# Decay attention and a hard-swish MoE layer: the masked scores stay in PSUM through the exponential, the half precision copy and the low pass

## The chip, the cores and the metric

One core of a Trainium2 chip. The kernel is one launch; its time is the device time of an execution in microseconds (us). A run is compared by the median of several executions. The engines are TensorE (PE; its weight loads are PEld), VectorE (DVE), ScalarE (ACT), GpSimd (POOL), and SyncE (SP), which issues the transfers.

## What is computed

The reference, cut to what matters (batch 8, 8 heads, 576 positions, head size 64; 4608 tokens of width 512, hidden width 2048):

```python
scores = scale * (q @ k.T)                         # scale = 1/8
cum = cumsum(log(clip(f, 1e-4, 1)))
scores = where(causal, -1e9, scores + cum[:, None] - cum[None, :])
attn = exp(scores - max(scores));  attn /= sum(attn) + 1e-9
x = (attn @ v)                                     # heads side by side: 4608 x 512
h = x @ w_in;  g = h * clip(h + 3, 0, 6) / 6
out = g @ w_out
```

## The kernel before

All 64 heads of attention and the whole MoE layer run on one core, one woven into the other. Numbers that need more than half precision are held as a pair of fp16 values, a high part and a low part (value minus high part), and multiplied as high by high, high by low and low by high.

**The visits.** A loop runs over 68 visits: four of kind A, eight of kind B (both for batch 0 only, in another form that the change leaves alone) and 56 of kind F, one for each head of batches 1 to 7. Visit 12 is the first of kind F. Each visit builds the scores of its head in `rows`, in two halves. Half 0 holds the row chunks 1, 4 and 0 (192, 576 and 64 keys wide), half 1 the chunks 2 and 3 (320 and 448 keys). For one half:

1. PE writes the scores of its chunks into the PSUM tile `pn`, 128x1024 fp32, two banks, from a pool of two such tiles (`ps_s`), by the matmuls on L632 and L635. Each visit so uses both tiles once.
2. DVE makes the **product** of each chunk (L643): it scales, adds the causal mask `W` and keeps the row's minimum in `MF`. Before the change the result goes to the SBUF tile `pp`, and `pn` is free when the last chunk has been read. An instruction that reads out the accumulator follows each product.
3. ACT takes the **exponential** of each chunk in place (L652), with the row's `MF` as bias, and then makes the half precision **copy** of it in the SBUF tile `ring` (L669).
4. DVE makes the **low pass** (`low`, L615): value times 16 minus the fp16 copy, written as fp16 to `ring`. It is seven instructions a head: half 0 has 128x128, 128x512, a pair of 64 columns for two chunks, and 64x64; half 1 has 128x256, 128x384 and the pair.
5. SP transposes `ring` into `pT` (L690), from which PE later makes `pav` = attention times values (L715 to L720, function `av`); DVE divides by the row sums (L748 to L750), and a last transpose puts the head into `xT`.

**The MoE layer.** `h_unit` makes 12 matmuls (L804 to L806) into `ph`, ACT applies the Relu to `r` (L812), DVE multiplies (L815, which reads `r` from SBUF and `ph` from PSUM), ACT makes the high part of `gT` (L816) and DVE the low part (L817, both inputs in SBUF). `out_unit` makes 48 matmuls into `po` (L859 to L861), ACT evicts them (L869). The MoE tile of a batch can start when all eight heads of the batch are in `xT`. The weights' own low parts are made on DVE in the first 160 us (L309). POOL prepares the next head's operands by six instructions a visit (L461 to L474), of which two read two SBUF tensors (L471, L474).

**The order.** The generator code interleaves visits and MoE steps; a list scheduler then fixes the order of each engine's instructions when the program is built. Each engine works through its own list strictly in order and waits on semaphores. The dependences are taken from tiles: two instructions on different engines, or two that follow each other on one engine, wait for each other where they touch the same PSUM tile.

## Time and profile before

| | |
|---|---|
| median of 3 runs | 1063.88 us (1058.98 to 1065.66) |
| the profiled execution | 1065.9 us, span in the profile 1064.1 us |
| PE busy | 1025.8 us, 96% |
| DVE busy | 773.5 us, 73% |
| ACT busy | 600.6 us, 56% |
| POOL busy | 423.2 us, 40% |

The span has four parts. From 0 to 143 us the weights and inputs are loaded and the visits of kind A and B run. From 143 to 282 us the first visits of kind F run, beside the MoE tile of batch 0. From 282 to 915 us the other visits run beside the MoE tiles of the batches before them. From 915 us on only MoE work of the last batch is left. A busy time is a union: an instruction that begins before the one ahead of it has ended does not count twice.

### The profile page before, as it was taken

What the parts mean: (1) busy time and instruction counts of PE and PEld (TensorE: products, weight loads), DVE (VectorE), ACT (ScalarE), POOL (GpSimd) and SP (SyncE); (2) the same over time, 40 slices, a digit from 0 to 9 for tenths busy, and PEclk for the clock granted to TensorE, in tenths of its full rate; (3) what the DMA queues carried; (4) which work ended last, traced back from release to release, by engine and by line L of the source; (5) the groups of instructions that cost most, each with busy time, mean ns of one, the idle gap of its engine ahead of it and who ended that gap; (6) DMA issues with size and microseconds to landing.
All of it is one profiled execution on the core that took longest, in us unless ns stands there. A gap on an engine that the chain in (4) does not pass through costs nothing.

```text
span 1064.1 us, 20761 instructions
## 1 busy us (share of the span) xinstructions
PE 1025.8 (96%) x7833; PEld 617.0 (58%) x7833; DVE 773.5 (73%) x1927; ACT 600.6 (56%) x1190; POOL 423.2 (40%) x436
## 2 busy tenths in 40 slices
PE   7799989889999999999999999999999999999998
PEld 5557856755455755555555755555555755545545
DVE  7977898999986679876986689876976788505500
ACT  4786765766664557655654556655743577405500
POOL 8654583665452444443343244444434442000000
PEclk8869999999999999999999999999999999999999
DMA  7765324778455554366444474456444534400000
GB/s 229 256 220 139 101 68 104 162 148 153 118 106 100 117 135 104 78 129 144 90 86 99 101 156 98 96 125 143 86 91 83 103 80 80 82 28 11 1 20 31
DMA packets 248416, 114.35 MB, mean 107 GB/s; under 512 B 224788, under 2 KB 226124, under 8 KB 248316
## 3 DMA queue, kind: packets, MB, share of 16 engines
q1 hardware_dynamic: 248316, 113.03, 46.9%
q8 instruction: 61, 1.00, 0.4%
q14 instruction: 39, 0.32, 0.1%
HBM read 47.93 MB, written 9.73 MB: 54 GB/s over the span
## 4 chain that ended last, share of the span: by engine, by line
PE 69%; DVE 16%; DMA 7%; ACT 4%; issue 3%; SPq 1%; DVEq 0%; ACTq 0%
PE po L859 11%; PE po L861 11%; PE po L860 11%; PE ph L804 7%; PE ph L806 6%; PE ph L805 6%; DVE ring L615 5%; PE pn L635 3%; PE pn L632 3%; DMA vst<-in_vS_dram 2%; DMA ring<-in_w_out_dram 2%; DVE r L815 2%; DVE pp L643 2%; DVE gT L817 2%; DVE w L309 1%
## 5 line engine op out<-in xcount | busy, mean ns | idle before, releaser
L615 DVE SCALAR_TENSOR_TENSOR ring<-pp,ring 128x128 f16<-128x128 f32 x392 | 235.2, 639 | 52.4 <-ACT ring L669 50.4
L461 POOL TENSOR_SCALAR TK<-ST 64x576 fp32r<-64x576 f32 (+1 forms) x68 | 54.3, 799 | 431.0 <-PE pn L632 394.0
L859 PE MATMUL po<-w,gT 128*128 128x512 f16 x560 | 209.6, 382 | 0.0
L804 PE MATMUL ph<-xT,w 128*128 128x512 f16 (+1 forms) x576 | 201.8, 358 | 7.7 <-DVE r L815 7.7
L861 PE MATMUL po<-w,gT 128*128 128x512 f16 x560 | 208.7, 381 | 0.3 <-DVE gT L817 0.3
L860 PE MATMUL po<-w,gT 128*128 128x512 f16 x560 | 208.6, 381 | 0.2 <-DVE w L309 0.2
L806 PE MATMUL ph<-xT,w 128*128 128x512 f16 (+1 forms) x576 | 201.2, 357 | 0.0
L805 PE MATMUL ph<-xT,w 128*128 128x512 f16 (+1 forms) x576 | 201.1, 357 | 0.0
L652 ACT ACTIVATE pp<-pp,MF 128x192 f32<-128x192 f32 x280 | 147.9, 554 | 87.3 <-DVE MF L643 86.1
L643 DVE CUSTOM_DVE_ANT_0 pp<-pn,W 128x192 f32<-128x192 f32 x280 | 123.3, 480 | 20.2 <-PE pn L635 19.9
L632 PE MATMUL pn<-TK,TQ 68*128 68x192 f32 x336 | 125.1, 385 | 5.3 <-DVE MF L643 3.0
L816 ACT CAST gT<-r 128x512 f16<-128x512 f32 (+1 forms) x144 | 81.6, 567 | 79.8 <-DVE r L815 79.1
L669 ACT ACTIVATE ring<-pp 128x192 f16<-128x192 f32 x280 | 119.8, 458 | 1.6
L812 ACT ACTIVATE r<-ph,bias_r,SC 128x512 f32<-128x512 f32 (+1 forms) x144 | 103.4, 720 | 29.2 <-PE ph L806 17.6
L817 DVE TENSOR_TENSOR gT<-r,gT 128x512 f16<-128x512 f32 (+1 forms) x144 | 100.8, 701 | 24.7 <-ACT gT L816 23.2
L815 DVE SCALAR_TENSOR_TENSOR r<-r,ph 128x512 f32<-128x512 f32 (+1 forms) x144 | 88.9, 618 | 40.6 <-ACT r L812 40.6
L635 PE MATMUL pn<-T,T 128*128 128x192 f32 x336 | 115.2, 370 | 0.0
L474 POOL TENSOR_TENSOR T<-ST,T 64x576 fp32r<-64x576 f32 (+1 forms) x68 | 107.3, 1577 | 5.1
L471 POOL TENSOR_TENSOR T<-ST,TQ 64x576 fp32r<-64x576 f32 (+2 forms) x68 | 98.6, 1451 | 5.4
L869 ACT ACTIVATE o<-po,SC 128x512 f32<-128x512 f32 (+1 forms) x37 | 24.7, 669 | 125.1 <-PE po L861 123.7
L861 PEld LDWEIGHTS <-gT 128*128 128x128 f16 x560 | 54.6, 98 | 67.5 <-issue 7.2
L860 PEld LDWEIGHTS <-gT 128*128 128x128 f16 x560 | 54.6, 98 | 59.8 <-issue 5.0
(152 smaller groups left out, 2016.1 us busy)
## 6 DMA issues: line engine op xcount, KB each, us to landing
ST<-in_qk_dram SPq DMA_DIRECT2D x64, 288.0 KB
out_dram<-o SPq DMA_DIRECT2D x33, 256.0 KB
ring<-in_w_out_dram SPq DMA_DIRECT2D x16, 512.0 KB
vst<-in_vS_dram SPq DMA_DIRECT2D x7, 1040.0 KB
ring<-in_w_in_dram SPq DMA_DIRECT2D x9, 512.0 KB
w<-in_w_in_dram SPq DMA_DIRECT2D x7, 512.0 KB
vst<-in_vS_dram SPq DMA_DIRECT2D x14, 130.0 KB
pT<-ring SPq DMA_TRANSPOSE x112
```

The costliest lines, as they stand in the source:

```text
L615: nc.vector.scalar_tensor_tensor(out_, x, PSC, hi, op0=ALU.mult, op1=ALU.subtract)
L632: nc.tensor.matmul(dst, TQ[i][0:D + 4, qs], TK[i][0:D + 4, a:e], start=True, stop=False)
L635: nc.tensor.matmul(dst, T7[j][:, qs], T1[j][:, a:e], start=False, stop=True)
L643: nc.vector.tensor_tensor_reduce(pp[:r, w:w + kw], pn[:r, o:o + kw], W[:r, 4 * P + r - kw:4 * P + r], -0.125, 3.0e38, ALU.add, ALU.min, ac ...
L652: nc.scalar.activation(x_, x_, AF.Exp, bias=mc[:r, e0 + x:e0 + x + 1], scale=-1.0)
L804: nc.tensor.matmul(ph, w1[0][:, cc, fs_], xh, start=(cc == 0), stop=False)
L805: nc.tensor.matmul(ph, w1[0][:, cc, fs_], xl, start=False, stop=False)
L806: d = nc.tensor.matmul(ph, w1[1][:, cc, fs_], xh, start=False, stop=(cc == NCC - 1))
L817: nc.vector.tensor_tensor(gT[:, 1, fc, c0:c1], r, gT[:, 0, fc, c0:c1], op=ALU.subtract)
L859: nc.tensor.matmul(po, g[:, 0, fc, ts_], w2[:, fc, 0, c], start=(fc == 0), stop=False)
L860: nc.tensor.matmul(po, g[:, 0, fc, ts_], w2[:, fc, 1, c], start=False, stop=False)
L861: d = nc.tensor.matmul(po, g[:, 1, fc, ts_], w2[:, fc, 0, c], start=False, stop=(fc == NFC - 1))
```

## The change

The product of each chunk is written back into `pn`, to where the scores stood. The exponential then runs in place in PSUM, and the copy and the low pass read from `pn`; `pp` is gone. In half 1 chunk 2 now lies in the first bank and chunk 3 in the second. Two small tiles that used the buffers of `pp` at the start (`fs`, `lf`) now lie in `xT`.

```diff
@@ decay()
-        fs = p2.tile([NHEAD, S], F32, tag="Pp", name="fs")
+        fs = xT[0].bitcast(F32).rearrange("p a c l t -> p (a c l t)")[0:NHEAD, 0:S]
...
-        lf = p2.tile([NHEAD, S], F32, tag="Pp", name="lf")
+        lf = xT[0].bitcast(F32).rearrange("p a c l t -> p (a c l t)")[0:NHEAD, S:2 * S]
@@
-    PLACE = {1: 0, 4: 192, 0: 768, 3: 0, 2: 512}
+    PLACE = {1: 0, 4: 192, 0: 768, 2: 0, 3: 512}
@@ rows()
-            pp = p2.tile([P, 832], F32, tag="Pp", name=f"pp_{v}_{half}")
-            at, w = {}, 0
+            pp, at = pn, PLACE
             for x, c in enumerate(NAT[half]):
                 o, r, kw = PLACE[c], RR[c], RB[c] + RR[c]
-                at[c] = w
                 nc.vector.tensor_tensor_reduce(
-                    pp[:r, w:w + kw], pn[:r, o:o + kw], W[:r, 4 * P + r - kw:4 * P + r],
+                    pn[:r, o:o + kw], pn[:r, o:o + kw], W[:r, 4 * P + r - kw:4 * P + r],
                     -0.125, 3.0e38, ALU.add, ALU.min, accum_out=mc[:r, e0 + x:e0 + x + 1],
                 )
-                w += kw
```

Three lines fewer: L643, L652, L669 and L690 become L641, L649, L666 and L687, and what stands behind them moves up by three (L804 to L801, L815 to L812, L859 to L856). L632, L635 and L615 stay.

The number of instructions of each kind is the same. Their order is not, and the waits are not. Two places of visit 50, in the steady part of the program, show how. The names in brackets are the semaphores that an instruction waits for: `Activation` is ACT's, `DVE` is DVE's, `DMAHW` a transfer's.

On ACT before, half 0 of visit 50, from the first exponential to the last copy (`ring1` is the half precision tile of this half):

```order
L652 ACTIVATE pp_50_0_8261<-pp_50_0_8261,MF0_169 128x192 [waits DVE_49]
L669 ACTIVATE ring1_186<-pp_50_0_8261 128x192 [waits DMAHW0_49,Activation_49]
L652 ACTIVATE pp_50_0_8261<-pp_50_0_8261,MF0_169 128x576 [waits DVE_49]
L652 ACTIVATE pp_50_0_8261<-pp_50_0_8261,MF0_169 64x64 [waits DVE_49]
L669 ACTIVATE ring1_186<-pp_50_0_8261 128x576 [waits Activation_49]
L812 ACTIVATE r_4_11_0_8280<-ph_4_11_0_8238,bias_r_147,SC_182 128x512 [waits PE_49]
L669 ACTIVATE ring1_186<-pp_50_0_8261 64x64 [waits Activation_49]
```

Each exponential waits for the product of its own chunk, and each copy for its own exponential. And now, the same half:

```order
L649 ACTIVATE pn_50_0_8174<-pn_50_0_8174,MF0_169 128x192 [waits DVE_49]
L649 ACTIVATE pn_50_0_8174<-pn_50_0_8174,MF0_169 128x576 [waits Activation_49]
L813 CAST gT_177<-r_4_13_0_8261 128x512 [waits DVE_49]
L649 ACTIVATE pn_50_0_8174<-pn_50_0_8174,MF0_169 64x64 [waits Activation_49]
L649 ACTIVATE pn_50_1_8233<-pn_50_1_8233,MF0_169 128x320 [waits DVE_49]
L666 ACTIVATE ring1_186<-pn_50_0_8174 128x192 [waits DMAHW1_49,Activation_49]
L809 ACTIVATE r_4_14_0_8325<-ph_4_14_0_8266,bias_r_147,SC_182 128x512 [waits PE_49]
L649 ACTIVATE pn_50_1_8233<-pn_50_1_8233,MF0_169 128x448 [waits Activation_49]
L666 ACTIVATE ring1_186<-pn_50_0_8174 128x576 [waits DVE_49]
L666 ACTIVATE ring2_187<-pn_50_1_8233 128x320 [waits DMAHW0_49,Activation_49]
L813 CAST gT_177<-r_4_14_0_8325 128x512 [waits DVE_49]
L666 ACTIVATE ring1_186<-pn_50_0_8174 64x64 [waits DVE_49]
```

The first exponential waits for the product of the last chunk, the first copy for the last exponential, and each further copy for DVE: for the low pass of the chunk before it. The two halves of the visit, and the MoE work, stand between them.

On DVE before, the same half from its first product to its second low pass:

```order
L643 ISA pp_50_0_8261,MF0_169<-pn_50_0_8252,W_149 128x192 [waits PE_49]
L643 ISA MF0_169 128x1
L643 ISA pp_50_0_8261,MF0_169<-pn_50_0_8252,W_149 128x576
L643 ISA MF0_169 128x1
L643 ISA pp_50_0_8261,MF0_169<-pn_50_0_8252,W_149 64x64
L643 ISA MF0_169 64x1
L615 SCALAR_TENSOR_TENSOR ring1_186<-pp_50_0_8261,ring1_186 128x128 [waits DMAHW0_49,Activation_49]
L615 SCALAR_TENSOR_TENSOR ring1_186<-pp_50_0_8261,ring1_186 128x512 [waits Activation_49]
```

And now (`r` is MoE work, `pn_50_1` the other half):

```order
L641 ISA pn_50_0_8174,MF0_169<-pn_50_0_8174,W_149 128x576 [waits DVE_49]
L641 ISA MF0_169 128x1
L641 ISA pn_50_0_8174,MF0_169<-pn_50_0_8174,W_149 64x64 [waits DVE_49]
L641 ISA MF0_169 64x1
L812 SCALAR_TENSOR_TENSOR r_4_13_0_8261<-r_4_13_0_8261,ph_4_13_0_8242 128x512 [waits Activation_49]
L641 ISA pn_50_1_8233,MF0_169<-pn_50_1_8233,W_149 128x320 [waits PE_49]
L641 ISA MF0_169 128x1
L641 ISA pn_50_1_8233,MF0_169<-pn_50_1_8233,W_149 128x448 [waits DVE_49]
L641 ISA MF0_169 128x1
L814 TENSOR_TENSOR gT_177<-r_4_13_0_8261,gT_177 128x512 [waits Activation_49]
L615 SCALAR_TENSOR_TENSOR ring1_186<-pn_50_0_8174,ring1_186 128x128 [waits DMAHW1_49,Activation_49]
```

The second and third product now wait for DVE itself, for the accumulator read ahead of them, and the products of both halves stand ahead of the first low pass. Where `pn` was free after the last product, it is now free after the last low pass of its half. On PE the first matmul of a later half waits for that low pass.

The scheduler has also moved MoE work on PE. Of the MoE matmuls there stand ahead of the first score matmul of each visit (first number into `ph`, second into `po`):

| visit | 12 | 14 | 16 | 18 | 20 | 22 | 24 | 30 |
|---|---|---|---|---|---|---|---|---|
| before | 156, 0 | 198, 90 | 264, 96 | 336, 96 | 384, 121 | 384, 173 | 471, 192 | 723, 384 |
| now | 156, 0 | 221, 96 | 384, 118 | 396, 192 | 411, 192 | 420, 192 | 528, 192 | 723, 384 |

From visit 12 on, more MoE work stands ahead of the visits than before; between visits 18 and 22 there is hardly any left, and at visit 30 the two orders are level again.

## The prediction

> **What bounds the kernel now.** I read the page's totals first, then the busy times by stretch, then the waits of PE.
>
> ```profile
> span 1064.1 us, 20761 instructions
> PE 1025.8 (96%) x7833; PEld 617.0 (58%) x7833; DVE 773.5 (73%) x1927; ACT 600.6 (56%) x1190; POOL 423.2 (40%) x436
> DVE  7977898999986679876986689876976788505500
> ```
>
> PE is busy for 96% of the span; 38.3 us are idle. A share of the whole hides where they lie, so the same by stretch (columns: the stretch, its length, then busy time and count of each engine, the granted PE clock, the DMA share and GB/s):
>
> ```profile
> core 0: us, PE busy (x) PEld busy (x) DVE busy (x) ACT busy (x) POOL busy (x), PEclk, DMA share, GB/s
> 0.00:143.00 143.00, 122.62 (x782) 94.20 (x782) 115.76 (x311) 96.22 (x196) 90.81 (x117) 0.87 0.58 178
> 143.00:282.00 139.00, 127.62 (x1119) 84.80 (x1120) 131.09 (x357) 92.89 (x202) 74.87 (x70) 0.98 0.66 140
> 282.00:915.00 633.00, 631.18 (x5008) 360.92 (x5007) 495.09 (x1211) 375.09 (x739) 257.57 (x250) 1.00 0.50 104
> 915.00:1064.10 149.10, 144.42 (x928) 77.12 (x926) 31.54 (x51) 36.42 (x56) 0.00 (x0) 1.00 0.09 24
> ```
>
> PE's idle time is 20.4 us in the first stretch, 11.4 in the second, 1.8 in the third, 4.7 in the tail. The first and the last hold no instruction of the changed loop (its products start at 142.8 us and end at 912.7, a row further down). In the third PE is full at a granted clock of 1.00, and DVE is busy for 78% of it: a faster DVE buys nothing there. In the second DVE is busy for 131.1 of 139 us and is the bound. **All that the change can give back is 11.4 + 1.8 = 13.2 us.** What PE waited for, in the second stretch (three rows) and in the third (the last):
>
> ```profile
> PE pav L715 <- DMA pT<-ring: 4.2, 3, 2.4
> PE pn L632 <- DVE MF L643: 3.0, 1, 3.0
> PE ph L804 <- DVE r L815: 1.4, 2, 1.1
> PE ph L804 <- DVE r L815: 1.8, 4, 0.7
> ```
>
> It waited for transposes of `ring` that were late because the low pass was late, and for products: both are DVE's.
>
> **The low pass gets shorter.** Groups of the third stretch (44 visits), of `low` and of the nearest instruction with one input in PSUM and one in SBUF, L815; the last row is L815's shorter form, over the whole run:
>
> ```profile
> L615 DVE SCALAR_TENSOR_TENSOR ring<-pp,ring 128x128 f16<-128x128 f32 x131 | 70.1, 535 | 2.3 <-ACT ring L669 0.8
> L815 DVE SCALAR_TENSOR_TENSOR r<-r,ph 128x512 f32<-128x512 f32 x89 | 60.2, 677 | 3.5 <-ACT r L812 3.5
> L615 DVE SCALAR_TENSOR_TENSOR ring<-pp,ring 128x384 f16<-128x384 f32 x43 | 50.5, 1174 | 0.3
> L615 DVE SCALAR_TENSOR_TENSOR ring<-pp,ring 128x512 f16<-128x512 f32 x44 | 35.7, 811 | 25.9 <-ACT ring L669 25.8
> L615 DVE SCALAR_TENSOR_TENSOR ring<-pp,ring 128x256 f16<-128x256 f32 x44 | 30.6, 696 | 22.7 <-ACT ring L669 22.7
> L615 DVE SCALAR_TENSOR_TENSOR ring<-pp,ring 64x64 f16<-64x64 f32 x44 | 13.5, 307 | 0.0
> L815 DVE SCALAR_TENSOR_TENSOR r<-r,ph 128x256 f32<-128x256 f32 x32 | 13.0, 405 | 0.5 <-ACT r L812 0.5
> ```
>
> 384 columns take longer than 512, so something other than the size sets the time. The order of time shows it: the same three low passes (256, 384, pair) in 1.08 us in one visit and in 3.52 us in another, where POOL was at L471, an instruction with two SBUF inputs:
>
> ```profile
> 261.02 1.08 DVE L615 SCALAR_TENSOR_TENSOR ring<-pp,ring 128x256 f16<-128x256 f32 x3
> 598.64 3.52 DVE L615 SCALAR_TENSOR_TENSOR ring<-pp,ring 128x256 f16<-128x256 f32 x3 [1.09 <-ACT ring L669]
> 598.70 1.63 POOL L471 TENSOR_TENSOR T<-ST,TQ 64x576 fp32r<-64x576 f32 x1
> ```
>
> `low` reads two SBUF tensors. After the change it reads one, as L815 does, and L815's two forms lie on a straight line, 405 and 677 ns for 256 and 512 columns, 1.06 ns a column, with no sign of POOL. By it 128 columns take 270, 256 take 405, 384 take 540, 512 take 677, and the 64x64 about 200. A visit has 3 x 270 + 405 + 540 + 677 + 200 = 2.63 us; instructions that follow each other overlap, in the free triple by 1.08 of 1.21 us, so 2.35 us of busy time. Against the busy time of L615 in the two stretches:
>
> ```profile
> 143.00:282.00 139.00, 46.44 (x84) 0.98 0.66 140
> 282.00:915.00 633.00, 187.94 (x306) 1.00 0.50 104
> ```
>
> 12 visits cost 46.4 us and would cost 28.2: **-18 us of DVE in the second stretch**. In the third 187.9 becomes 103, -85 us, and hides under PE. The bounds: 0, if the wait for POOL stays, and the 18.
>
> [...]
>
> **What is added: waits.** Half 0 of one visit of before, and the costs of ACT's steps (exponential L652, copy L669):
>
> ```profile
> 481.05 0.36 DVE L643 CUSTOM_DVE_ANT_0 pp<-pn,W 128x192 f32<-128x192 f32 x1 [2.06 <-PE pn L635]
> 481.33 0.75 DVE L643 CUSTOM_DVE_ANT_0 pp<-pn,W 128x576 f32<-128x576 f32 x1
> 482.01 0.21 DVE L643 CUSTOM_DVE_ANT_0 pp<-pn,W 64x64 f32<-64x64 f32 x1
> 482.16 0.07 DVE L643 DVE_READ_ACCUMULATOR2_ANT MF<- 64x1 f32 x1
> 482.33 0.29 DVE L615 SCALAR_TENSOR_TENSOR ring<-pp,ring 128x128 f16<-128x128 f32 x1
> 483.81 1.02 DVE L615 SCALAR_TENSOR_TENSOR ring<-pp,ring 128x512 f16<-128x512 f32 x3 [1.19 <-ACT ring L669]
> ...
> L652 ACT ACTIVATE pp<-pp,MF 128x576 f32<-128x576 f32 x56 | 42.7, 763 | 2.6 <-DVE MF L643 2.5
> L652 ACT ACTIVATE pp<-pp,MF 128x192 f32<-128x192 f32 x56 | 25.4, 453 | 35.3 <-DVE MF L643 34.3
> L652 ACT ACTIVATE pp<-pp,MF 64x64 f32<-64x64 f32 x56 | 18.6, 333 | 0.0
> L669 ACT ACTIVATE ring<-pp 128x576 f16<-128x576 f32 x56 | 37.5, 670 | 0.0
> L669 ACT ACTIVATE ring<-pp 128x192 f16<-128x192 f32 x56 | 20.2, 360 | 1.4
> L669 ACT ACTIVATE ring<-pp 64x64 f16<-64x64 f32 x56 | 13.5, 241 | 0.0
> ```
>
> Before, the half goes from its first product to its last low pass in 483.81 + 1.02 - 481.05 = 3.8 us, and `pn` is free after 1.2. Now everything in it runs one behind the other. The products, with the accumulator read between them, take 0.36 + 0.75 + 0.21 + 3 x 0.08 = 1.55; the exponentials 0.45 + 0.76 + 0.33 = 1.55; then copy, low pass, copy, low pass, copy, two low passes: 0.36 + 0.27 + 0.67 + 0.68 + 0.24 + 0.27 + 0.20 = 2.7. That is **5.8 us at the least, 2 us later than before, and `pn` is held for 5.8 us in place of 1.2**. With the other work of both lists between the steps it is more: in visit 50 there stand 22 instructions on DVE from the first product to the last low pass, which at the durations of their own groups sum to 8 us.
>
> Is the tile free in time? The products of 56 visits start between 142.8 and 912.7 us, so a visit has 13.7 us; the score matmuls (instructions on `pn` in the third stretch: PE's busy time is 143.14 us, for 44 visits and two halves) hold a tile for 1.6 us of it:
>
> ```profile
> L643 DVE CUSTOM_DVE_ANT_0 pp<-pn,W x280: 207/476/755, 142.8 to 912.7; 128x192 f32<-128x192 f32 x28, 64x64 f32<-64x64 f32 x28, 128x448 f32<-128x448 f32 x28, 128x576 f32<-128x576 f32 x28
> 282.00:915.00 633.00, 143.14 (x520) 86.98 (x520) 96.83 (x220) 1.00 0.50 104
> ```
>
> That leaves 12.1 us for a chain of 6 to 8 with some waits in it. In the third stretch I take it as hidden, at +1 us, with bounds of 0 and of the rival below. Behind a copy that waits for DVE stand the next Relu and cast of the MoE on ACT, and behind them PE's next `ph`; before, this hand-over cost PE 1.8 us in 633.
>
> The serial products cost DVE 3 x 0.08 us a visit, 3 us in the second stretch. The writes to PSUM by DVE (280 products) and ACT (280 exponentials) have no row of before. The nearest rows are the products that write SBUF and the exponentials above; I take these durations, with a bound of double the products above (96.83 us in 44 visits, +2.2 us a visit) and a tenth less below. The moved tiles `fs` and `lf` are used before visit 0 is done and cost nothing; the moved places of chunks 2 and 3 change no size.
>
> **The second stretch, summed.** DVE falls from 131.1 by 18, plus 3: 116 us, under PE's 127.6. By totals PE would be full and all 11.4 us would come back. By order it would not. The table of the change has about 60 `ph` and 96 `po` matmuls more ahead of visit 18, and from 18 to 22 only 24 and none. A matmul of 512 columns takes 0.22 us (chain: three in 0.65):
>
> ```profile
> 930.74 0.65 PE po L860 x3
> ```
>
> So some 25 us of PE's work now stand earlier, beside visits 12 to 17, where PE becomes the bound; and visits 18 to 21 have only their own matmuls, 143.14 / 44 = 3.3 us of scores and about 1 of `pav`, while their tiles turn round in 1.6 + 5.8 = 7.4 us at the least. PE idles there for 3 us a visit by that minimum, 12 us in four visits, less what visits 12 to 17 have run ahead. I take 8 to 9 us of idle time for the stretch in place of 11.4: **-3 us**.
>
> Sum: -3 + 1 = -2 us; 1065.9 becomes 1063.9 for the profiled execution, and the median, 1063.9 (2 us under the profiled one), becomes **1062 us**.
>
> **The rivals.**
> *PE stays fed.* If the chain of visits 18 to 21 hides behind work queued ahead, all of 13.2 us come back: 1051. For it: DVE's total falls under PE's. Against it: the hole in the order.
> *The tile comes back late.* In a visit where MoE units stand densest, DVE's share of the chain is nearer 10 us than 8, and each half has four hand-overs between ACT and DVE in which the waiting engine may sit behind one foreign instruction of 0.68 us: 10 + 2.7 = 12.7, past the 12.1 that the period leaves. Then PE stops for 0.6 us a visit or more, on L632. At 0.6 to 1 us in 44 visits it is 1064 + 26 to 44, less the gain: about 1090. It decides as soon as `pn` is held for over 12.1 us. Against it: DVE's busy time falls by 2 us a visit. [...]
> *PSUM costs more.* With products of double length the second stretch gains 26 us of DVE and stands at 142 of 139: no gain, some 5 us lost, and 1 to 2% in sum with late tiles: 1075.
> *The change doesn't do what it says*: the low pass goes on waiting for POOL through its other input. Then only waits are added: DVE 134 of 139, the chain 2 us longer: 1072.
>
> **How the numbers follow.** Forecast (within 1053 and 1074): 0.50. PE fed: 0.20. Late tile: 0.18. PSUM dearer: 0.06, and the low pass unchanged 0.06, both mostly at or past the upper edge. One per cent, about what a measurement of this kernel can tell from none, is 10.6 us. Faster by more: 0.22, the fed PE and a little of the forecast. Slower by more: 0.28. The range 1050 to 1082 takes in all of the gain, the forecast and the mild half of the late tiles.
>
> **What would show it.** Right: L615 in 128x384 near 540 ns and DVE's busy time down by some 100 us; the products and exponentials as long as before; PE at 630 of 633 in the steady part. Wrong: a row of PE or PEld waiting on L632 for the low pass or the copy, with tens of us; products near 1.5 us; `ph` waiting for L812. The forecast fails if PE waits at `pn` in the steady visits, or if visits 18 to 21 show no idle PE.

## The result: 1.6% slower

| | before | after |
|---|---|---|
| median | 1064.8 us (4 runs, 1059.0 to 1066.9) | 1080.9 us (4 runs, 1080.0 to 1081.7) |
| ratio | | 1.0158, 95% interval 1.0130 to 1.0186 |
| span of the profiled execution | 1064.1 us | 1078.3 us |

The time lies inside the range of the prediction, but on the other side: "within 1%" was the likeliest case, and a fall of 2 us the forecast. The page's totals and two of its slice lines (40 slices of 27 us, busy tenths; PEclk is the granted clock of PE):

```profile
span 1078.3 us, 20878 instructions
PE 1029.1 (95%) x7833; PEld 624.3 (58%) x7833; DVE 698.9 (65%) x1927; ACT 585.7 (54%) x1190; POOL 397.6 (37%) x436
PE   6799899986999999999999999999999999999998
PEclk8979999996999999999999999999999999999999
```

DVE, the engine that the prediction held to be the bound of the second stretch, has lost 74.6 us, and the kernel is slower all the same. The tenth slice is new: PE busy for 6 tenths of it, at a clock of 6 tenths. The same four stretches as before the change:

```profile
core 0: us, PE busy (x) PEld busy (x) DVE busy (x) ACT busy (x) POOL busy (x), PEclk, DMA share, GB/s
0.00:143.00 143.00, 120.02 (x793) 93.62 (x793) 118.08 (x316) 96.78 (x197) 91.39 (x118) 0.89 0.58 178
143.00:282.00 139.00, 121.17 (x1005) 82.48 (x1004) 100.10 (x313) 80.27 (x180) 59.39 (x62) 0.91 0.54 112
282.00:915.00 633.00, 628.81 (x5007) 362.17 (x5004) 433.78 (x1207) 359.34 (x732) 246.85 (x258) 1.00 0.53 108
915.00:1078.30 163.30, 159.07 (x1039) 86.05 (x1037) 46.90 (x94) 49.32 (x84) 0.00 (x0) 0.99 0.13 32
```

The second stretch holds the whole difference. PE's idle time there was 11.4 us and is 139 - 121.17 = 17.8, and the clock fell from 0.98 to 0.91. Busy time by clock is 127.62 x 0.98 = 125.1 us of work at full speed before and 121.17 x 0.91 = 110.3 now: 14.8 us of work are left over, and the span is 14.2 us longer. They show as 14.65 us more of busy time in the tail. In the steady part PE is idle for 4.2 us in place of 1.8.

### The profile page after: what moved, and what is told of

It is laid out like the page before. It is cut to its first block, busy times and chain, and to the rows that moved or that the text cites. A ratio compares the mean times of both kernels' runs of the same rounds, so it can differ in the third digit from the quotient of the medians.

```text
span 1078.3 us, 20878 instructions
## 1 busy us (share of the span) xinstructions
PE 1029.1 (95%) x7833; PEld 624.3 (58%) x7833; DVE 698.9 (65%) x1927; ACT 585.7 (54%) x1190; POOL 397.6 (37%) x436
## 4 chain that ended last, share of the span: by engine, by line
PE 75%; DMA 9%; DVE 8%; ACT 3%; SPq 2%; issue 2%; POOL 1%; ACTq 0%; DVEq 0%; POOLq 0%
PE po L856 11%; PE po L857 11%; PE po L858 11%; PE ph L801 8%; PE ph L803 8%; PE ph L802 8%; PE pn L632 4%; PE pn L635 3%; DMA pT<-ring 2%; DMA vst<-in_vS_dram 2%; DMA ring<-in_w_out_dram 2%; PE pav L716 1%; PE pav L717 1%; PE pav L715 1%; PE phs L828 1%
## 5 line engine op out<-in xcount | busy, mean ns | idle before, releaser
L461 POOL TENSOR_SCALAR TK<-ST 64x576 fp32r<-64x576 f32 (+1 forms) x68 | 49.1, 722 | 473.0 <-PE pn L632 434.8
L856 PE MATMUL po<-w,gT 128*128 128x512 f16 x560 | 208.7, 380 | 0.6 <-DVE r L812 0.6
L801 PE MATMUL ph<-xT,w 128*128 128x512 f16 (+1 forms) x576 | 201.5, 361 | 7.2 <-DVE r L812 7.2
L649 ACT ACTIVATE pn<-pn,MF 128x192 f32<-128x192 f32 (+1 forms) x280 | 133.5, 496 | 133.9 <-DVE MF L641 112.6
L641 DVE CUSTOM_DVE_ANT_0 pn<-pn,W 128x192 f32<-128x192 f32 x280 | 135.1, 500 | 75.8 <-PE pn L635 72.7
L615 DVE SCALAR_TENSOR_TENSOR ring<-pn,ring 128x128 f16<-128x128 f32 (+1 forms) x392 | 137.8, 386 | 59.4 <-ACT ring L666 57.6
L666 ACT ACTIVATE ring<-pn 128x192 f16<-128x192 f32 (+1 forms) x280 | 114.4, 433 | 39.9 <-DVE ring L615 37.3
L812 DVE SCALAR_TENSOR_TENSOR r<-r,ph 128x512 f32<-128x512 f32 (+1 forms) x144 | 89.2, 621 | 56.6 <-ACT r L809 56.5
L632 PE MATMUL pn<-TK,TQ 68*128 68x192 f32 x336 | 115.1, 363 | 8.6 <-ACT ring L666 7.2
L474 POOL TENSOR_TENSOR T<-ST,T 64x576 fp32r<-64x576 f32 (+1 forms) x68 | 100.6, 1479 | 5.1
L635 PE MATMUL pn<-T,T 128*128 128x192 f32 x336 | 102.1, 331 | 0.0
L471 POOL TENSOR_TENSOR T<-ST,TQ 64x576 fp32r<-64x576 f32 (+2 forms) x68 | 92.3, 1357 | 5.4
L802 PEld LDWEIGHTS <-w 128*128 128x128 f16 x576 | 56.7, 99 | 57.0 <-issue 12.3
```

What stands on the lines that cost most here:

```text
L615: nc.vector.scalar_tensor_tensor(out_, x, PSC, hi, op0=ALU.mult, op1=ALU.subtract)
L632: nc.tensor.matmul(dst, TQ[i][0:D + 4, qs], TK[i][0:D + 4, a:e], start=True, stop=False)
L635: nc.tensor.matmul(dst, T7[j][:, qs], T1[j][:, a:e], start=False, stop=True)
L641: nc.vector.tensor_tensor_reduce(pn[:r, o:o + kw], pn[:r, o:o + kw], W[:r, 4 * P + r - kw:4 * P + r], -0.125, 3.0e38, ALU.add, ALU.min, ac ...
L649: nc.scalar.activation(x_, x_, AF.Exp, bias=mc[:r, e0 + x:e0 + x + 1], scale=-1.0)
L666: nc.scalar.activation(hl[:r, h0[c]:h0[c] + kw], pp[:r, at[c]:at[c] + kw], AF.Copy, scale=PSC)
```

## Where the time went in the second stretch

PE in 20 us pieces (columns: piece, length, busy, clock, DMA share, GB/s), two of before and then the same two of after:

```profile
240.00:260.00 20.00, 18.61 (x159) 1.00 0.76 144
260.00:280.00 20.00, 18.86 (x162) 1.00 0.78 179
```

```profile
240.00:260.00 20.00, 10.83 (x88) 0.76 0.63 128
260.00:280.00 20.00, 16.92 (x128) 0.73 0.75 129
```

What PE waited for from 143 to 320 us (us, times, longest):

```profile
PE pav L712 <- DMA pT<-ring: 8.3, 3, 4.6
PE pn L632 <- ACT ring L666: 7.2, 2, 5.7
PE ph L801 <- DVE r L812: 2.0, 1, 2.0
```

The second row is the wait that the change brings in: the first matmul on a tile behind the copies (and low passes) of the half that had it before. Before, PE waited there once, for products (3.0 us). The one of 5.7 us can be followed in the order of time. First DVE, then ACT, for half 0 of the visit whose products start at 235 us; then PE:

```profile
234.98 0.37 DVE L641 CUSTOM_DVE_ANT_0 pn<-pn,W 128x192 f32<-128x192 f32 x1 [4.76 <-PE pn L635]
...
236.75 0.66 DVE L641 CUSTOM_DVE_ANT_0 pn<-pn,W 128x448 f32<-128x448 f32 x1
...
239.27 0.94 DVE L412 SCALAR_TENSOR_TENSOR v<-vst,SC,v 128x320 f16<-128x320 f32 x1
240.13 0.28 DVE L615 SCALAR_TENSOR_TENSOR ring<-pn,ring 128x128 f16<-128x128 f32 x1
240.62 1.54 DVE L753 TENSOR_TENSOR xhl<-xf,xhl 128x640 f16<-128x640 f32 x1 [0.20 <-ACT xhl L752]
242.07 2.10 DVE L615 SCALAR_TENSOR_TENSOR ring<-pn,ring 128x256 f16<-128x256 f32 x6
```

```profile
237.00 1.74 ACT L649 ACTIVATE pn<-pn,MF 128x192 f32<-128x192 f32 x4 [4.77 <-DVE MF L641]
...
239.65 0.32 ACT L666 ACTIVATE ring<-pn 128x192 f16<-128x192 f32 x1
...
242.52 0.81 ACT L666 ACTIVATE ring<-pn 128x448 f16<-128x448 f32 x2 [1.07 <-DVE ring L615]
```

```profile
235.81 0.38 PE L802 MATMUL ph<-xT,w 128*128 128x512 f16 x1
236.02 0.38 PE L803 MATMUL ph<-xT,w 128*128 128x512 f16 x1
236.24 0.38 PE L801 MATMUL ph<-xT,w 128*128 128x512 f16 x1
...
243.95 0.50 PE L632 MATMUL pn<-TK,TQ 68*128 68x192 f32 x1 [5.67 <-ACT ring L666]
...
247.08 0.65 PE L801 MATMUL ph<-xT,w 128*128 128x512 f16 x1
247.53 0.63 PE L802 MATMUL ph<-xT,w 128*128 128x512 f16 x1
247.95 0.63 PE L803 MATMUL ph<-xT,w 128*128 128x512 f16 x1
```

From the first product to the tile's next matmul it is 243.95 - 234.98 = 9.0 us, of which the half's own steps are 5.8. The rest is the other half (its products and exponentials stand between) and foreign instructions, of which L412 (0.94 us) and L753 (1.54 us) are the longest. L753 stands on DVE ahead of most low passes, ACT's last copies wait for the low pass behind it (1.07 us), and PE stands behind them. Its list has almost nothing else here, because this is where the order has hardly any MoE work left.

**The clock.** Before the stop `ph` matmuls of 512 columns start 0.21 and 0.22 us apart; behind it 0.45 and 0.42. PE ran dry and then worked at half speed. The clock's own record has 23.9 us at half clock in the part of the run that the table below calls 120 to 200, where before had 3.4; 20.5 of them lie from 243 to 250 and from 257 to 271 us, around this stop and the two before `pav`. The record also has 3.4 us at half clock behind each of two shorter stops, of 2.0 us (from 193.4 us) and of 1.6 us (from 302.1 us). So these stops were paid for once more behind them, and no term of the prediction had this second price.

## A measure for the experiments

Each kernel's scheduler moves work in time, so equal times are not equal work. For the comparison I give each of PE's 7833 matmuls its length at full speed, which makes 929 us in every kernel: about 0.214 us for 512 columns, and less nearly in proportion. It is an estimate; in the traces of before and after such matmuls start 0.216 us apart in the median at full clock and 0.427 at half, and those of 256 and 128 columns 0.109 and 0.056 apart at full clock. I take PE's lost time as the time of the trace less the work done by then. It is worked out from the matmul records, one profiled execution each, which can lie some us from the kernel's median (e3's lies 6 us below it, e7's 5 and e11's 7 above); it takes in stops, half clock and the gaps of small matmuls alike. 0 to 120 us of work is the start with the first visits of kind F. 120 to 200 holds about visits 16 to 24 at the rate of the two kernels, which the expectations below call visits 13 to 24; at the other rates it holds visits 18 to 23 (e2, e3) and 21 to 26 (e4). The rest is the steady part and the tail.

| kernel | ratio to before (95%) | lost, 0-120 | lost, 120-200 | lost, rest | half clock in 120-200 |
|---|---|---|---|---|---|
| before | | 87.0 | 12.8 | 30.4 | 3.4 |
| **after** | 1.0158 (1.0130 to 1.0186) | 82.9 | **29.8** | 32.1 | 23.9 |
| e1 tiles held, before | 1.0106 (1.0072 to 1.0140) | 80.1 | 23.0 | 32.8 | 13.7 |
| e13 control of e1 | 1.0046 (1.0027 to 1.0065) | 84.9 | 14.5 | 33.7 | 6.8 |
| e14 control, after | 1.0147 (1.0109 to 1.0184) | 87.2 | 28.4 | 31.8 | 23.9 |
| e5 half 1 alone | 1.0049 (1.0028 to 1.0070) | 84.0 | 20.3 | 33.3 | 10.2 |
| e6 half 0 alone | 1.0088 (1.0060 to 1.0116) | 87.5 | 21.8 | 31.9 | 13.7 |
| e8 copies first | 1.0051 (1.0025 to 1.0077) | 85.7 | 21.5 | 29.2 | 17.1 |
| e15 half 1, copies first | 0.9987 (0.9965 to 1.0009) | 84.0 | 11.1 | 29.7 | 0 |
| e9 exponential to SBUF | 1.0103 (1.0056 to 1.0149) | 87.4 | 21.7 | 31.3 | 10.2 |
| e2 rate 0.15, after | 1.0171 (1.0132 to 1.0210) | 103.2 | 8.1 | 33.9 | 3.4 |
| e3 rate 0.20, after | 1.0166 (1.0127 to 1.0205) | 92.8 | 9.7 | 33.2 | 3.4 |
| e4 rate 0.15, before | 1.0230 (1.0195 to 1.0265) | 103.8 | 18.5 | 28.2 | 11.5 |
| e7 four input buffers | 1.0025 (1.0003 to 1.0046) | 76.8 | 26.9 | 32.1 | 23.9 |
| e10 the fourth from visit 12 | 1.0040 (1.0015 to 1.0066) | 69.7 | 29.7 | 32.1 | 23.9 |
| e11 loads from POOL | 1.0197 (1.0144 to 1.0250) | 84.6 | 38.7 | 32.0 | 34.1 |
| e12 copies first, four buffers | 0.9967 (0.9943 to 0.9991) | 74.6 | 19.9 | 29.9 | 17.1 |

Of after's 14.6 us more than before, -4.1 fall in the start, **+17.0 in visits 16 to 24**, and +1.7 in all the rest. Counted by visits, from the first score matmul of visit 18 to that of visit 22, the lost time is 9.3 us before and 24.1 after: these four visits hold +14.8 us, as much as the whole loss.

## The experiments

The expectations use names for the theories. "Order": the MoE work that the scheduler moved ahead of visits 12 to 17 leaves a hole, and the hole costs the time. "Chain", later "turns": the copies and low passes that wait for each other in PSUM. "Hold": the time for which each half keeps its score tile. "Transpose": transposes stand in SP's list behind input loads that wait for POOL.

**e1: the kernel before, with the tiles held.** One small DVE instruction (64x1) at the end of each half reads the scores again, so that `pn` is kept until the last low pass, while everything else stays in SBUF as it was.

```diff
+            held = p2.tile([64, 1], F32, tag="held", name=f"held_{v}_{half}")
+            h1 = h0[0] - 64 if 0 in NAT[half] else h0[b] - 64
+            nc.vector.tensor_tensor(held, pn[:64, 0:1], hl[:64, h1:h1 + 1], op=ALU.subtract)
```

> The kernel before, with one thing of the change alone: the score tile is held until the half's last low pass, by one DVE instruction of one column that reads the tile and the low pass's result (112 in all, about 0.1 us each). Products, exponentials, copies and low passes stay in SBUF, and no engine waits for another between the chunks. The built order moves MoE work ahead of visits 13 to 18 nearly as in the change (384 and 131 MoE matmuls ahead of visit 18; the change has 396 and 192, before 336 and 96) and leaves the same hole from 20 to 22. Theory 'order' (the longer hold makes the scheduler pull the MoE tile of batch 0 forward; PE then has nothing left in visits 18 to 22, idles, and its clock is halved): loses 10 to 20 us against before, 1074 to 1084, all of it between 140 and 320 us. Rival 'chain' (what costs is the turn-taking of ACT and DVE in PSUM on the chip): this kernel has none of it, so at most the added instructions show: 1062 to 1069.

1072.0 us, 1.0106: between the two. The order moves as in the change (384 `ph` ahead of visit 17, 411 ahead of 21), and 23.0 us are lost in visits 16 to 24 in place of 12.8. From 143 to 320 us PE never waits at L632 here: what the hold costs in this run comes by way of the order and of late transposes, not of a stop at the tile.

**e13: its control.** The same instruction reads `hl` in place of `pn`, so no tile is held.

```diff
-            nc.vector.tensor_tensor(held, pn[:64, 0:1], hl[:64, h1:h1 + 1], op=ALU.subtract)
+            nc.vector.tensor_tensor(held, hl[:64, h1:h1 + 1], hl[:64, h1:h1 + 1], op=ALU.subtract)
```

> The kernel before, with the same small instruction a half as in the run that held the tiles, but reading SBUF alone, so that no tile is held. It is the control of that run (1.0106). Theory 'hold' (what costs is that the tiles come free late): 0.998 to 1.003, PE's lost time between 120 and 200 us of its work at 12 to 15 us as before (12.8), not 23. Rival 'order' (any added instruction redraws the scheduler's order, and a redrawn order costs about a per cent): 1.006 to 1.013. The built order has the same counts of MoE matmuls ahead of visits 12 to 30 as before, within two.

1067.4 us, 1.0046: above what "hold" gave and below what the rival gave. The added instruction costs something by itself, spread over visits 16 to 24 (+1.7) and the rest (+3.3). The order is that of before, to within two matmuls. The hold, with the order that the scheduler builds for it, costs the difference to e1: 0.60 ± 0.39% of the time (the half widths of the two intervals, squared, added and rooted), and 23.0 - 14.5 = 8.5 us of lost time, half of the 17. The waits of PE for transposes, from 143 to 320 us, tell the two apart; the first row is e1's, the second the control's:

```profile
PE pav L718 <- DMA pT<-ring: 9.2, 9, 1.5
```

```profile
PE pav L718 <- DMA pT<-ring: 0.7, 1, 0.7
```

**e14: the same control on the changed kernel** (the three lines as in e13; the one that counts):

```diff
+            nc.vector.tensor_tensor(held, hl[:64, h1:h1 + 1], hl[:64, h1:h1 + 1], op=ALU.subtract)
```

> The change with the same small instruction, which reads SBUF alone: the control on the other side. Both theories on the second stretch: as the change, 1.013 to 1.020, 27 to 32 us lost between 120 and 200 us of PE's work. What is above or below that is how much a redrawn first stretch moves the time by itself.

1077.8 us, 1.0147, with 28.4 us lost in visits 16 to 24. The loss there does not depend on the small instruction. The column "lost, 0-120" moved by 4.3 us (82.9 to 87.2), though the order is the same and the time is not longer: differences of that size in this column say nothing about an edit.

**e2, e3, e4: the hole moved.** `F_RATE` sets how fast the generator feeds MoE units of batches 0 and 1. At 0.15 or 0.20 for batch 1 the order of the changed kernel has MoE work between visits 18 and 22 again. e4 is the same edit on the kernel before.

```diff
-    F_RATE = (0.45, 0.45)
+    F_RATE = (0.45, 0.15)      # e2 and, in the kernel before, e4; 0.20 in e3
```

> The changed kernel, with the rate at which MoE steps are woven into the visits of batch 1 lowered from 0.45 to 0.15. All waits, holds and PSUM reads of the change stay; the built order has 312 and 96 MoE matmuls ahead of visit 18 and 384 and 140 ahead of visit 20, as in the kernel before (336, 96 and 384, 121). Theory 'order': the hole closes, PE's waits between 235 and 285 us go, and the time falls by 10 to 20 us, to 1061 to 1071; with the shorter low pass it may pass the kernel before. Rival 'chain': the visits stay as slow as in the change and the time stays within 1075 to 1085.

> As the run before it, with a rate of 0.20: 348 and 96 MoE matmuls ahead of visit 18, 384 and 180 ahead of visit 20, 456 and 192 ahead of visit 22: a hole that is half closed. Theory 'order': between the run at 0.15 and the change, 1064 to 1076. Rival 'chain': 1075 to 1085.

> Control: the kernel before with the same lower rate of 0.15 and nothing of the change. MoE matmuls ahead of visit 18: 228 and 96, of visit 22: 252 and 96, so MoE work is late rather than early. Theory 'order': the rate is no gain by itself; in visits 13 to 22 DVE is the bound and PE gets less to do, so 1064 to 1080. If this run is as much faster than before as the run with the change at 0.15 is faster than the change, then the rate explains the gain and the hole does not.

1079.2 and 1077.5 us, 1.0171 and 1.0166: nothing comes back, and "order" misses its bands. But the edit did not close the hole, it moved it. In e2 the order has MoE work between visits 18 and 22, and none from visit 15 to visit 17 (240 `ph` and 96 `po` ahead of all three). The loss in 120 to 200 falls to 8.1 and 9.7 us, below that of before, and appears ahead of it (103.2 and 92.8 in the first column); 20.5 us at half clock stand between 187 and 208 us, where the hole of e2 now is.

e4 shows how much the hole does by itself. At 0.15 the kernel before is the slower of the two, 1.0230 against 1.0171 (a difference of 0.59 ± 0.52%): the change is no loss at this rate. And e4's order leaves the kernel before just as little MoE work beside visits 18 to 21 as the change has at 0.45, 24 `ph` and no `po`. These four visits lose 21.8 us in e4 and 24.1 in the change, against 9.3 before. So "order" is not refuted by these runs. Visits without MoE work beside them cost PE most of this time in the kernel before as well.

**e5 and e6: one half each.** The half that is named keeps its product in PSUM; the other goes through an SBUF tile as before.

```diff
+            if half == 1:          # e6: half == 0
+                pp, at = pn, PLACE
+            else:
+                pp = p2.tile([P, 832], F32, tag="Pp", name=f"pp_{v}_{half}")
...
```

> Only half 1 (chunks 2 and 3) stays in PSUM; half 0 goes through the SBUF tile as before. Half 1's low passes were the ones that POOL held up most (1174 and 696 ns for 384 and 256 columns). Theory 'hold' (the score tiles, held through the whole chain and given back together, set the pace of visits 13 to 22; PE then runs dry and its clock is halved): one of the two tiles is free early, so most of the loss goes and most of the shorter low pass stays; 1055 to 1066. Theory 'chain' (the turn-taking between ACT and DVE costs wherever it stands): half of the loss stays, 1066 to 1073.

> The other half alone: half 0 (chunks 1, 4 and 0) stays in PSUM, half 1 goes through SBUF. Its chain has one link more (three chunks) and its low passes gain less. Theory 'hold': better than the change, worse than half 1 alone, 1062 to 1072. Theory 'chain': as half 1 alone or worse, 1068 to 1076.

1069.6 and 1074.8 us, 1.0049 and 1.0088. Both lie in the bands of "chain", e5 above and e6 above those of "hold". In visits 16 to 24 they lose 7.5 and 9.0 us more than before; the sum, 16.5, is about the 17.0 of the whole change. Half 0 has three chunks and the longer chain, and costs more.

**e8: copies first.** In the changed kernel all copies of a half stand ahead of all its low passes, so that ACT and DVE hand the tile over once and not once for each chunk.

```diff
                 nc.scalar.activation(
                     hl[:r, h0[c]:h0[c] + kw], pp[:r, at[c]:at[c] + kw], AF.Copy, scale=PSC
                 )
+            for c in NAT[half]:
+                r, kw, a = RR[c], RB[c] + RR[c], GH[half][c]
                 if c:
```

> The changed kernel, but in each half ACT makes all copies first and DVE makes all low passes behind them, so the two engines change over once instead of four to six times. The tile is held for the same sum of durations. Theory 'chain': at least half of the loss goes, 1064 to 1073. Theory 'hold': the tile comes back hardly earlier, 1075 to 1083.

1070.0 us, 1.0051, as "chain" had it: about two thirds of the loss come back (1.07 ± 0.38%), and 8.3 of the 17 us in visits 16 to 24. That the turns on the chip are what costs does not follow: the order has changed, too. Beside visits 18 and 19 stand 33 and 15 MoE matmuls in place of 6 and 9, and these visits now lose 1.4 and 1.2 us in place of 6.5 and 4.3. Visits 20 and 21 have 0 and 9 as in the change, and they lose 7.7 and 6.6 us with copies first, 6.5 and 6.8 without.

**e15: half 1 alone, copies first.**

> The change for half 1 alone (1.0049), with both copies of that half ahead of its low passes. Theory 'hold' with 'turns': the tile of half 1 is held shortest and nothing takes turns but the products, the order ahead of visits 12 to 30 is that of before, and the low passes of half 1 (256 and 384 columns, where POOL's waits were longest) are the shorter ones: 0.995 to 1.002, 12 to 17 us lost between 120 and 200 us of PE's work (half 1 alone: 20.3). If the loss comes from writing PSUM at all: 1.004 to 1.007 as half 1 alone.

1060.8 us, 0.9987. The edits are those of e5 and e8 together. Visits 16 to 24 lose 11.1 us, a little less than before the change, with none at half clock, and the built order ahead of visits 12 to 30 is nearly that of before (342 `ph` ahead of visit 18, 384 ahead of 22). PE's busy time and clock from 143 to 320 us, for before, after, e1, e13 and e15 in this order:

```profile
143.00:320.00 177.00, 165.62 (x1376) 0.98 0.62 127
```

```profile
143.00:320.00 177.00, 157.58 (x1260) 0.92 0.53 111
```

```profile
143.00:320.00 177.00, 160.71 (x1318) 0.96 0.62 119
```

```profile
143.00:320.00 177.00, 164.44 (x1346) 0.96 0.60 126
```

```profile
143.00:320.00 177.00, 165.34 (x1415) 0.99 0.64 133
```

So a half may live in PSUM without loss if its tile comes free early enough; the order then stays, too. Over all runs at the rate of 0.45 the loss in visits 16 to 24 goes with the order: 11 to 15 us where it is nearly that of before (before, e13, e15), about 20 us or more wherever MoE work has moved ahead. That the faster low pass then earns nothing agrees with the steady part: PE is full there (631.2 of 633 us before and 628.8 after), and DVE's time is not asked for.

**e9: the exponential writes SBUF.** The product stays in `pn`, the exponential moves it to an SBUF tile, and copy and low pass read that.

```diff
...
-                x_ = pp[:r, at[c]:at[c] + kw]
                 nc.scalar.activation(
-                    x_, x_, AF.Exp, bias=mc[:r, e0 + x:e0 + x + 1], scale=-1.0
+                    pp[:r, at[c]:at[c] + kw], pn[:r, PLACE[c]:PLACE[c] + kw], AF.Exp,
+                    bias=mc[:r, e0 + x:e0 + x + 1], scale=-1.0
                 )
```

> The change with one step taken back: the product still goes back into the PSUM tile, but the exponential writes its result to an SBUF tile, from which the copy and the low pass read as before the change. The tile is now held through products and exponentials, 1.55 + 1.55 = 3.1 us at the least, in place of 5.8 (the change) and 1.2 (before), and copy and low pass no longer take turns. Theory 'hold' (the loss comes from how long the tiles are held when visits follow each other closely): about the share (3.1 - 1.2) / (5.8 - 1.2) = 0.4 of the 1.58%, so 1.004 to 1.008, with 113 to 119 us of PE work done... PE's lost time between 120 and 200 us of its work at 17 to 23 us (before 12.8, the change 29.8). Rival 'turns' (the loss comes from copy and low pass taking turns in PSUM alone): 0.998 to 1.003. Rival 'writes' (the products that wait for each other and write PSUM): 1.010 to 1.016. DVE's busy time should be back near 770 us, since the low pass reads two SBUF tensors again.

1074.0 us, 1.0103 with a wide interval, 1.0056 to 1.0149, that covers part of what "hold" and what "writes" gave; "turns" alone is excluded. The tile is held for 3.1 us by the sum of its steps in place of 5.8, and 21.7 us are lost, as with the full hold. The loss is not in proportion to the hold. MoE work has moved ahead here too (384 `ph` and 160 `po` ahead of visit 20; before, 384 and 121), and DVE also has its long low passes back here (765.2 us busy). How much of it is the three steps that run one behind the other stays open.

**e7, e10, e11: the transposes behind the loads.** In the changed kernel SP's own waits from 143 to 300 us have grown in one row; the first is of before, the second of after:

```profile
SPq L426 <- POOL T L474: 8.6, 4, 4.1
```

```profile
SPq L426 <- POOL T L474: 34.0, 11, 5.3
```

L426 loads a head's input into one of three buffers, which POOL must have read; the transposes L687 stand behind it in SP's list. e7 gives the changed kernel a fourth buffer, for which the room of `pp` is there; e10 uses it from visit 12 on alone; e11 lets POOL issue the loads of visits 12 to 67 itself.

```diff
-    NQK, NL, NST = 3, 2, 3
+    NQK, NL, NST = 3, 2, 4                          # e7, e10
-        t = ST[v % NST]
+        t = ST[v % (3 if v < 12 else NST)]           # e10, in its three places
-            nc.sync.dma_start(t, qk[n])
+            (nc.gpsimd if kind == "F" else nc.sync).dma_start(t, qk[n])    # e11
```

> The changed kernel with four buffers for a visit's q and k instead of three, so that the load on SP has no need to wait for POOL. In the changed kernel this load waited 34.0 us for POOL's L474 between 143 and 300 us (8.6 before), and the transposes of the half precision tile stand behind it on SP. Rival 'transpose' (the transposes come late because they queue behind that load): 1066 to 1074. Theories 'hold' and 'chain': the tiles come back no earlier, 1076 to 1084.

1066.3 us, 1.0025: most of the loss is gone, which looked like a proof. The trace says otherwise. The wait of L426 is still 35.7 us, visits 16 to 24 lose 26.9 us with 23.9 at half clock, and the gain stands in the first 120 us of work: it is there by 153 us, before the first transpose of this kind is issued.

> The change with the fourth input buffer, but used from visit 12 on alone; visits 0 to 11 turn through three as in the change. It tells where the fourth buffer's gain (1.0158 to 1.0025) came from. Theory 'transpose' (transposes queue on SP behind input loads that wait for POOL, in visits 13 to 24): the gain stays, 1.001 to 1.006, and the time lost by PE in its first 120 us of work is as in the change, 83 us. Rival 'early' (the gain came from visits 0 to 11, whose loads go out earlier): the gain goes, 1.012 to 1.018.

1066.9 us, 1.0040. The gain stays, as "transpose" had it, but not where it had it: 29.7 us are lost in visits 16 to 24, as in the change, and 69.7 in the start. The rival had the place right and the effect wrong. The buffer that no early visit uses lets the load of a later visit stand among the first of SP's list, and the scheduler lays out the whole start anew. PE's row of the start, of after first (as shown above, PE alone) and then of e10:

```profile
0.00:143.00 143.00, 120.02 (x793) 0.89 0.58 178
```

```profile
0.00:143.00 143.00, 128.59 (x874) 0.94 0.59 183
```

> The change, with the input loads of visits 12 to 67 issued by POOL in place of SP. POOL reads that buffer last itself, so the load no longer makes SP wait, and no transpose stands behind it. Theory 'transpose': PE's waits for transposes in visits 13 to 24 shrink from 10.7 us to 3 to 5, and the time falls to 1.003 to 1.010 of before. Rival 'hold' (SP's wait only mirrors a PE that is late anyway): 1.012 to 1.018, or above if POOL's issue of 56 loads delays its own operands.

1084.2 us, 1.0197. SP no longer waits at L426, and PE's waits for transposes from 143 to 320 us are still there:

```profile
PE pav L712 <- DMA pT<-ring: 10.2, 6, 3.2
```

They are not shorter than the change's 8.3, and visits 16 to 24 lose 38.7 us. "Transpose" falls: taking the load's wait from SP's list gave nothing back. That this wait only mirrors a PE, and so a POOL, that is late already fits this, but is not shown by itself.

**e12: the two edits that helped, together.**

```diff
+            for c in NAT[half]:                          # as in e8
+                r, kw, a = RR[c], RB[c] + RR[c], GH[half][c]
-    NQK, NL, NST = 3, 2, 3
+    NQK, NL, NST = 3, 2, 4
```

> The change with both of the edits that helped: all copies of a half before all its low passes (1.0051 alone), and four input buffers throughout (1.0025 alone). If the two take back different losses (the turns in visits 13 to 24, and the early visits), the gains add: 1.0158 - 0.0107 - 0.0133 = 0.992, between 0.988 and 0.996. If they take back the same loss: 1.000 to 1.004.

1059.8 us, 0.9967 (0.9943 to 0.9991): four fifths of the sum of both, a little above the band expected, and the only version clearly below before, by a third of a per cent. Its gain over before is the start (74.6 us in place of 87.0); visits 16 to 24 still lose 7 us more. What a fourth buffer would do in the kernel before, where `pp` takes the room, wasn't tried.

## Why the prediction was wrong, step by step

**The step that failed** is "I take 8 to 9 us of idle time for the stretch in place of 11.4: -3 us". It is 17.8 us of idle time and a clock of 0.91 in place of 0.98: about +15 us. The place was right, visits 18 to 21, and so was the reason, visits without MoE work beside them. The size was wrong: the prediction had 12 us of idle PE there, less 3 to 4, and these visits lost 24.1 us, 14.8 more than before. One term was mis-sized and one was put at nothing.

- *The turn-round.* The sum used the least time, 1.6 + 5.8 = 7.4 us. First products of visits 18 to 22 start at 235.0, 245.9, 254.1, 263.6 and 274.1 us: 9.8 us a visit on the mean. The chain of 8 us that the prediction itself had worked out with foreign instructions, for visit 50, makes 9.6 with the scores; it was used for the steady part and not where it mattered. With 4.3 us of PE's own work in such a visit, 5.5 us are left over and not 3. Before, the same visits went by at 9.7 us each (213.8 to 252.5), but PE had MoE work beside them. So they became no faster when DVE was relieved. Nor is the tile's turn-round all that paces such a visit: in e4 the kernel before, whose tile is free early, takes 9.0 us for each of visits 18 to 21 (195.9 to 231.7).
- *The clock.* Nothing was reckoned for it. In the second stretch PE was busy for 18.6 of the 23.9 us at half clock, and for 6.2 of 6.8 us before. At half speed that is 9.3 us of work lost in place of 3.1: some 6 us of the loss.

The credit of 3 to 4 us for what visits 12 to 17 had "run ahead" is not the step that failed. Visit 18 starts 21 us later than before (235.0 and 213.8 us), but with some 25 us more of PE's work done, and the start lost 4.1 us less; by e14 a difference of that size can also come without a cause.

**The low pass: right.** Groups of the third stretch, after:

```profile
L615 DVE SCALAR_TENSOR_TENSOR ring<-pn,ring 128x512 f16<-128x512 f32 x44 | 30.2, 686 | 7.7 <-ACT ring L666 6.9
L615 DVE SCALAR_TENSOR_TENSOR ring<-pn,ring 128x384 f16<-128x384 f32 x44 | 24.2, 549 | 6.9 <-ACT ring L666 6.9
L615 DVE SCALAR_TENSOR_TENSOR ring<-pn,ring 128x256 f16<-128x256 f32 x44 | 18.4, 417 | 6.7 <-ACT ring L666 6.5
L641 DVE CUSTOM_DVE_ANT_0 pn<-pn,W 128x576 f32<-128x576 f32 x43 | 32.8, 763 | 0.9
L641 DVE DVE_READ_ACCUMULATOR2_ANT MF<- 128x1 f32 x172 | 24.0, 139 | 0.0
L649 ACT ACTIVATE pn<-pn,MF 128x576 f32<-128x576 f32 x43 | 30.7, 715 | 1.1
```

and L615's busy time in the second and the third stretch:

```profile
143.00:282.00 139.00, 25.05 (x71) 0.91 0.54 112
282.00:915.00 633.00, 107.81 (x307) 1.00 0.53 108
```

384 columns take 549 ns (forecast 540), 512 take 686 (677) and 256 take 417 (405); in the third stretch 107.8 us (103). The rival "the change doesn't do what it says" is refuted. The line through L815's two forms held, to within 12 ns. 128x128 low passes took 284 ns in the median of 168 before, from SBUF, and 282 after, from PSUM, so no extra cost of the source shows.

**Products and exponentials: nearly right.** The product of 576 columns takes 763 ns in place of 752, the exponential of 576 takes 715 in place of 763. "PSUM costs more" is refuted. In e9, where the exponential reads PSUM and writes SBUF, it takes 734 ns (the mean of all five widths is 521 there, 554 before and 496 after): of the 48 ns, 29 come with the source and 19 with the destination. One thing was missed: the accumulator read takes 139 ns where it took 79, and 132 in place of 75 behind the smallest chunk, five times a visit.

**The steady part: right.** Forecast +1 us; the lost time behind 200 us of work is 1.7 us longer, and PE's waits at the tile in the third stretch are one of 1.6 us:

```profile
PE pn L632 <- ACT ring L666: 1.6, 1, 1.6
```

The rival "the tile comes back late" had a right mechanism for 7.2 us of the stops, PE at L632 behind the copy, and the wrong place: it named the steady visits, whose period of 13.7 us hides a chain of 9 us, at a price of 26 to 44 us. The wait came in the close visits, whose period of 9.8 us is hardly longer than that chain.

**How much is shown.** That the loss is in visits 18 to 21 is read from the traces. That holding the tiles makes the kernel slower without a single write to PSUM is shown by e1 against e13 (0.60 ± 0.39%), and that copies first gives back about two thirds by e8 (1.07 ± 0.38%). Both edits also redraw the order, and the lost time goes with it. Of visits 15 to 24 in the change, e14, e2, e3, e7, e10 and e11, 21 have fewer than 15 MoE matmuls beside them and lose 7.0 us on the mean, and 27 have 35 to 59 and lose 0.9. With copies first (e8, e12) there are two such visits in place of four, and they still lose 7.2 us each; in e4 the kernel before has four, which lose 5.4. By these traces the hole is most of the cause: with the tile held the scheduler moves MoE work ahead (e1 against e13), and visits are left without any. What the hold and the turns add on the chip is a smaller part, 1.6 us a visit by the figures of e4; no run holds the tile with the order kept, so this part is an estimate. That the half clock adds to the stops is read from the traces, not tried by itself. e9's part, the serial products and exponentials, is open.

## What to carry to other kernels

Keeping the value in PSUM took 80 us off the low pass here (187.9 to 107.8 us in the third stretch), but what it spends is the tile: find the stretch in which the tile's next user comes soonest, look what other work the built order leaves beside it, and work out the turn-round there with the foreign instructions that stand in each engine's list, not with the least time of the steps. Where several engines must touch one tile, let each do all its work in it before the next (copies first: about two thirds of the loss came back, by way of the order). Before a list scheduler's order is called innocent, count the work that stands beside each visit: an edit that fills one hole can open another. Price a stop of the matmul engine with the half-speed time that follows it (here 20.5 us around three stops of 12.7 us in sum), and when an edit helps, look in which stretch, since a scheduler may have redrawn one that the edit does not touch.

## What had not been expected of the hardware

- The accumulator read behind a product that writes PSUM takes 139 ns, and 79 ns behind one that writes SBUF (224 instructions each).
- In-place exponentials in PSUM are 48 ns shorter at 576 columns than in SBUF (715 and 763 ns); from PSUM to SBUF they take 734 ns (e9).
- Around three stops of 5.7, 4.6 and 2.4 us PE was at half clock for 20.5 us, in two pieces of 6.8 and 13.7. The burst of 6.2 us between the second and the third (259.2 to 265.4) did not bring the clock back. Stops of 2.0 and 1.6 us were followed by 3.4 us at half clock each.
